# Held loads of v, other engines for copies and adds, and other places for the steps of the front in a fused attention and feed-forward kernel

## The chip, the cores and the metric

The kernel runs on one core of a Trainium2 chip. The metric is the time of one execution in microseconds (us) of device time. Below, TensorE is also called PE (PEld is its weight load), VectorE DVE, ScalarE ACT, GpSimd POOL and SyncE SP, as in the profile.

## What is computed

q, k and v have the shape (8 batches, 8 heads, 576 positions, 64), in float32. Each head has a local attention (a position sees those less than 4 away) and a coarse one (q, k and v averaged over groups of 4 positions, full attention over the 144 groups, the result repeated 4 times). Their sum is the input of a two-layer network with an ELU:

```python
q_d = q.reshape(B, H, Sd, 4, D).mean(axis=3)              # k_d, v_d alike
out_up = np.repeat(sm_attn(q_d, k_d, v_d), 4, axis=2)     # coarse part
scores = np.where(np.abs(pos[:, None] - pos[None, :]) < 4, scale * q @ k.T, -1e9)
out_local = softmax(scores) @ v                           # local part
x = (out_up + out_local).transpose(0, 2, 1, 3).reshape(4608, 512)
h = x @ w_in                                              # 512 -> 2048
out = np.where(h > 0, h, np.exp(np.minimum(h, 0)) - 1) @ w_out   # 2048 -> 512
```

## The kernel before, in words

The attention works on pairs of heads (four pairs, j = 0 to 3, in each batch b), the network on blocks of 512 rows of x (t = 0 to 8). All is issued in one program whose order is written out by hand: `at(time, function, ...)` files a step under a planned time, and at the end (L935) the steps are issued in the order of these times. The times are places in an order, not clock times; each engine then works through its own queue in that order and waits where an input is not there. A move in the tables F, PLAN, MM1 and MM2 therefore moves every instruction of a step in the queues of all engines at once.

The front (tables F and FK, L842 and L843) is batch 0 up to the first matmuls of the network. Its steps are, by the letter of the table:

- T, `first_transposes`: PE transposes q and k of a pair and makes their sums over 4; ACT or DVE copies the four results (qt, kt, qd, kd) out of PSUM. S and Z, `first_scores`: the scores of the first and the second half of the positions, and the exponentials on ACT (0.89 us each).
- V, `first_v`: sums of v over 4 (vs) and their copy (vd). D: denominators and their reciprocals on DVE. P, `first_spread`: the reciprocals spread over the partitions (rb) and copied (rcb).
- O and N: the outputs (lg), scaled on DVE (ln, L568); then the coarse part is added to the local one (L574, on DVE or POOL by a list), which fills x transposed (xt).
- H, `ahead`: the first matmuls of the network (hp, L619). lv, lw, cv: loads of v of batch 0 and 1 and the casts of v (POOL, L242). rp: loads of q and k of batch 1 that cast on the way (POOL's queue, L166). wi: the loads of w_in (POOL's queue, L137). lists `load_wo`: those of w_out (L141).

FK holds numbers of filler matmuls and transposes on zeros (`keep`, L679 and L682), which are issued ahead of a step on PE. Three PSUM tiles (`two`) are passed round between scores, spread reciprocals and outputs, two after `close_front`, so one of these steps waits until the tile of an earlier one has been read.

Then the network runs beside the attention of later batches. mm1 of block 0 is done in 16 parts; each ends in an exponential on ACT (e, L644) and two instructions on DVE (L645 and L646, gt). mm2 (op, L660) needs gt and w_out: the first four groups of four matmuls need the four quarters of w_out in turn. Loads of q, k and v from HBM go through SP's queue, and those with a cast through POOL's. Some loads are held: a memset of one element of the target (L176, L217) makes the load wait until DVE has come to it.

Of the kernel before, what the change touches and what calls it, by code (L numbers as in the profile page):

```python
# [69 lines left out]
def kernel(  # L70
# [9 lines left out]
    nc = tc.nc  # L80
# [131 lines left out]
    def load_v(b, j):  # L212
# [3 lines left out]
        if b == 1:  # L216
            nc.vector.memset(t[0:1, 1, 0:1], 0.0)  # L217
# [346 lines left out]
    def normalise_half(js, g, lg):  # L564
# [7 lines left out]
        for t, a, b_, to in parts:  # L572
            eng = nc.vector if t == 0 and [1, 1, 1, 0, 0, 0, 0, 1][2 * g + js[0] // 2] else nc.gpsimd
# [6 lines left out]
    def normalise(b, j, lg):  # L580
# [14 lines left out]
        while t0 < S * (b + 1):  # L595
# [7 lines left out]
            eng = nc.vector if (b, t) == (1, 1) and [1, 1, 1, 0, 0, 0, 0, 1][4 + j] else nc.gpsimd  # L603
# [80 lines left out]
    def first():  # L684
# [3 lines left out]
        keep(t, 13)  # L688
# [76 lines left out]
    def first_transposes(j, fill):  # L765
        transposes(0, j, fill)
        s, copy = st[(0, j)], dve if [0, 1, 1, 0][j] else act
# [24 lines left out]
    def first_spread(i, n):  # L792
        js, g = halves(i)
        rb = two("rb")
        keep(rb, n)
        spread_half(js, g, rb)
        w = HB + SH
        (dve if [0, 0, 0, 1][i] else act)(
            out=RB[0][:, js[0] : js[1] + 1, w * g : w * g + w], in_=g2(rb[:], 0, w)
        )  # L800

    def first_v(j):
        v_first(0, j, dve if [0, 0, 0, 0][j] else act)
# [38 lines left out]
    F = dict(T=[-41.13, -39.95, -36.66, -32.16], S=[-39.2, -35.63, -33.39, -30.84], Z=[-32.52, -32.14, -32.14, -28.4], V=[-33.32, -30.92, -30.71, -27.94], P=[-29.75, -28.02, -20.88, -18.53], O=[-30, -26.95, -20.73, -13.92], N=[-28.12, -24.72, -19.09, -13.8], H=[-24.18, -20.45, -18.09, -17.91], lv=[-52.45, -36.44, -34.49, -32.17], cv=[-36.2, -33.27, -32.43, -29.76], lw=[-30, -29.11, -20.29, -11.97], rp=[-28.54, -23.88, -22.41, -14.05], D=[-32.62, -29.37, -29.34, -24.56], wi=[-33.19, -32.56, -30.01, -29.05], cf=[-29.29], k=[-41.47, -35.38, -33.37, -28.21])  # L842
    FK = dict(Tq=[1, 0, 0, 0], Tk=[0, 0, 2, 0], S=[1, 0, 2, 1], Z=[1, 0, 2, 0], P=[0, 1, 0, 0], O=[1, 4, 0, 2], D=[0, 0, 0, 0])  # L843
# [29 lines left out]
    MM1 = [[-14.19, 1.09, 0.706], [19.14, 0.992], [35.73, 1.018], [51.52, 1.02]]  # L873
    MM2 = [[14.98, 0.794], [34.5, 1.095], [51.68, 1.02]]
# [13 lines left out]
    def load(n):  # L888
# [5 lines left out]
        1: dict(tr=[-12.21, -5.594, -1.76, -1.482], sc=[-7.07, 0.103, 0.888, 2.276], cast=[-23.96, -13.31, -12.32, 1.701], dn=[16.38], vs=[15.62], sp=[18.61, 18.14, 18.46, 18.98], out=[18.98, 18.52, 18.54, 18.99], so=[10.57], si=[10.03]),  # L894
# [72 lines left out]
```

## Time and profile before

| | us |
|---|---|
| median of 3 runs | 357.72 (356.89 to 359.48) |
| the profiled execution's own time | 356.68 |
| its span, first to last instruction | 354.8 |
| PE busy | 338.6 (95%) |
| DVE busy | 247.1 (70%) |
| ACT busy | 200.0 (56%) |
| POOL busy | 167.6 (47%) |

The profile is one execution. 1.88 us of its time lie outside the span. Times in it are counted from the start of the span. A queue named PEq, SPq and so on is the sequencer of the engine, which waits and issues DMAs. The chain of work is followed back from the last instruction to what released each; "issue" in it is time in which the engine waited for nothing that the profile shows.

### The profile page before, as it was taken

To read this page: it belongs to the slowest core of one execution; us is meant where nothing else is said; L and a number is where in the kernel's file an instruction comes from. 1 tells how busy PE (TensorE), PEld (TensorE's weight loads), DVE (VectorE), ACT (ScalarE), POOL (GpSimd) and SP (SyncE) were. 2 spreads that over 40 slices of the span, in tenths; PEclk is the share of its full clock that TensorE was granted. 3 is DMA by queue.
4 is the path that set the end of the run, shared out by engine and by line. 5 is a ranking of instruction groups with operands and counts; after the bars stand their busy time and mean duration, and the time that the engine had idled before them with its cause. 6 is when DMAs were issued, how large, how long until landed. Compare 5 with 4: busy or idle time off the path is not lost.

```text
span 354.8 us, 8863 instructions
## 1 busy us (share of the span) xinstructions
PE 338.6 (95%) x3520; PEld 191.6 (54%) x3520; DVE 247.1 (70%) x452; ACT 200.0 (56%) x368; POOL 167.6 (47%) x305
## 2 busy tenths in 40 slices
PE   8887998899979999999999999999999999999996
PEld 4665886555555555555555555555555544444443
DVE  2316998676898868887997799879766855555510
ACT  3572798457775754677476736773664444444421
POOL 4534658596877744954595459846200500000000
PEclk9998999999999999999999999999999999999999
DMA  8999999999794958686968698461004010010012
GB/s 180 179 191 200 189 201 217 226 216 229 170 203 92 228 147 164 144 219 152 188 166 217 151 179 202 110 142 35 31 32 117 32 59 30 31 59 30 31 59 89
DMA packets 100322, 49.12 MB, mean 138 GB/s; under 512 B 81770, under 2 KB 95290, under 8 KB 100282
## 3 DMA queue, kind: packets, MB, share of 16 engines
q1 hardware_dynamic: 94442, 42.20, 53.1%
q0 software_dynamic: 5600, 6.26, 10.6%
q8 instruction: 27, 0.44, 0.6%
q10 hardware_dynamic: 240, 0.11, 0.2%
q14 instruction: 13, 0.11, 0.1%
HBM read 42.24 MB, written 9.62 MB: 146 GB/s over the span
## 4 chain that ended last, share of the span: by engine, by line
PE 88%; DVE 5%; ACT 4%; issue 2%; DVEq 0%; ACTq 0%
PE op L660 35%; PE hp L640 31%; PE sc L382 3%; PE lg L531 2%; PE hp L619 2%; PE sc L679 2%; PE tqk L268 2%; ACT pex L402 1%; PE sc L392 1%; PE vs L338 1%; DVE ln L584 1%; DVE gt L646 1%; PE lg L539 1%; PE den L437 1%; ACT e L644 1%
## 5 line engine op out<-in xcount | busy, mean ns | idle before, releaser
L660 PE MATMUL op<-WO,gt 128*128 128x512 f16 (+2 forms) x592 | 145.3, 374 | 0.0
L644 ACT ACTIVATE e<-hp 128x512 f16<-128x512 f32 x144 | 86.3, 602 | 91.8 <-PE hp L640 78.2
L640 PE MATMUL hp<-xt,WI 128*128 128x512 f16 x512 | 132.0, 380 | 0.7 <-DVE xt L604 0.6
L646 DVE SCALAR_TENSOR_TENSOR gt<-hp,e 128x512 f16<-128x512 f32 x144 | 99.6, 692 | 6.4
L660 PEld LDWEIGHTS <-gt 128*128 128x128 f16 x592 | 55.2, 98 | 61.6 <-issue 0.9
L645 DVE TENSOR_SCALAR e<-e 128x512 f16<-128x512 f16 x144 | 60.1, 417 | 40.2 <-ACT e L644 39.5
L640 PEld LDWEIGHTS <-WI 128*128 128x128 f16 x512 | 55.0, 114 | 48.2
L604 POOL TENSOR_TENSOR xt<-ln 128x128 f16<-128x128 f16 (+10 forms) x62 | 37.4, 632 | 48.7 <-DVE ln L591 41.1
L402 ACT ACTIVATE pex<-sc 112x576 f16<-112x576 f32 x112 | 50.0, 528 | 10.6 <-PE sc L392 10.5
L329 POOL TENSOR_TENSOR t<-qt 128x288 f32<-128x288 f16 x27 | 18.2, 672 | 39.4 <-ACT qt L298 39.4
L422 DVE TENSOR_TENSOR pex<-pex,MASK 112x1152 f16<-112x1152 f16 x28 | 23.8, 851 | 15.5 <-ACT pex L402 15.3
L242 POOL CAST v<-v 112x768 f16<-112x768 f32 x32 | 27.0, 844 | 12.2 <-DMA v<-in_v_dram 12.2
L666 ACT COPY os<-op 128x512 f32<-128x512 f32 (+2 forms) x37 | 21.4, 578 | 18.3 <-PE op L660 18.1
L323 DVE TENSOR_REDUCE kd<-kt 128x144 f16<-128x576 f16 x28 | 20.8, 744 | 1.1 <-ACT kt L305 1.1
L298 ACT COPY qt<-tqk 128x576 f16<-128x576 f16 x28 | 18.0, 644 | 5.9 <-PE tqk L268 5.1
L205 POOL CAST k<-k 96x768 f16<-96x768 f32 x24 | 20.4, 848 | 0.1
L205 POOL CAST q<-q 96x768 f16<-96x768 f32 x24 | 19.7, 821 | 0.2 <-issue 0.2
L382 PEld LDWEIGHTS <-kt 64*112 64x112 f16 x336 | 11.3, 127 | 12.4 <-issue 11.6
L619 PE MATMUL hp<-xt,WI 128*128 128x256 f16 x128 | 17.0, 283 | 0.5 <-DVE v L217 0.4
L382 PE MATMUL sc<-qt,kt 64*112 64x96 f16 x336 | 14.7, 217 | 1.5 <-ACT pex L402 1.3
L331 POOL TENSOR_TENSOR qd<-t 128x144 f16<-128x144 f32 x27 | 14.0, 519 | 2.1
L591 DVE TENSOR_TENSOR ln<-lg,rcb 128x576 f16<-128x576 f32 x20 | 15.0, 748 | 0.0
(111 smaller groups left out, 291.5 us busy)
## 6 DMA issues: line engine op xcount, KB each, us to landing
v<-in_v_dram SPq DMA_DIRECT2D x30, 336.0 KB, 6.0
out_dram<-os SPq DMA_DIRECT2D x35, 256.0 KB, 2.1
q<-in_q_dram SPq DMA_DIRECT2D x25, 288.0 KB, 3.5
k<-in_k_dram SPq DMA_DIRECT2D x25, 288.0 KB, 4.3
rcb<-rd SPq DMA_DIRECT2D x10, 360.0 KB, 5.2
WI<-in_moe_w_in_dram POOLq DMA_DIRECT2D x4, 512.0 KB, 9.6
WO<-in_moe_w_out_dram POOLq DMA_DIRECT2D x4, 512.0 KB, 7.8
q<-in_q_dram POOLq DMA_DIRECT2D x7, 144.0 KB, 7.1
```

The costliest lines, as they stand in the source:

```text
L205: nc.gpsimd.tensor_copy(out=x[:], in_=src)
L242: nc.gpsimd.tensor_copy(out=v16[:], in_=v32[:].rearrange("p (e c) d -> p c e d", e=2))
L382: nc.tensor.matmul(sc[e][0:KW, a : a + QB], s["kt"][r, KO - PAD + QB * c :][:, 0:KW], s["qt"][c][r], start=True, stop=True,)
L402: nc.scalar.activation(out=s["p"][0:rows, e, :, a : a + n], in_=g2(sc[0:rows], a, n), func=AF.Exp, scale=SCALE / 16 if b and a == HB else ...
L422: nc.vector.tensor_tensor(out=to, in0=to, in1=mk2, op=AB.mult)
L604: eng.tensor_tensor(out=xt(t)[:, j, t0 - TBLK * t : t1 - TBLK * t], in0=ln[:, la : la + z - a], in1=_rep4(ln[:, ga : ga + (z - a) // 4]), ...
L619: nc.tensor.matmul(FS[i][:, 256 * f : 256 * f + 256], w_in(dc, 2 * n + f), xts[0][:, dc, 256 * h : 256 * h + 256], start=(f == dc == 0), s ...
L640: nc.tensor.matmul(hp, w_in(dc, fc), xts[t][:, dc, :], start=(dc == 0), stop=(dc == DMC - 1),)
L644: nc.scalar.activation(out=e, in_=hp, func=AF.Exp)
L645: nc.vector.tensor_scalar(out=e, in0=e, scalar1=1.0, scalar2=-1.0, op0=AB.min, op1=AB.add)
L646: nc.vector.scalar_tensor_tensor(out=to, in0=hp, scalar=0.0, op0=AB.max, in1=e, op1=AB.add)
L660: nc.tensor.matmul(op_[:, a:z], gts[t][:, fc, 128 * tt : 128 * tt + 128], WO[:, fc, a:z], start=(fc == 0), stop=(fc == FCN - 1),)
```

## The change

- v of batch 0 is now also loaded behind memsets on DVE (L216): its four loads leave SP's queue only when DVE has passed its casts of k of pair 0 and the mask; the fourth memset stands on a buffer that v of pair 0 must have left.
- The adds for the first two outputs (N of index 0 and 1) go from DVE to POOL. The copies of kt, qd and kd of pairs 1 and 2 go from DVE to ACT, those of vd of pairs 0, 1 and 3 from ACT to DVE, and the last copy of rcb of batch 0 from DVE to ACT.
- The steps of the front, of batch 1 and some of batches 2 and 3 get other places, and the fillers other numbers: 15 in place of 13 at the start, 20 transposes in place of 4 ahead of the first transposes, 4 ahead of k's.

In the order that results, PE's queue has T of pairs 0 and 1 first, then S of pair 0, T of pair 2, Z 0, S 1, V 0, Z 1, T 3, S 2, Z 2, D 0, V 1, S 3, O 0, P 0, D 1, Z 3, D 2, V 2, P 1, V 3, D 3, O 1, P 2, O 2, two of H, P 3, two of H, O 3, and then batch 1. POOL's queue has the third and the fourth quarter of w_out later: the fourth stands behind the casts of q, k and v of the first pair of batch 2.

```diff
--- before.py
+++ after.py
@@ -213,7 +213,7 @@
 
         t = V00 if (b, j) == (0, 0) else sb.tile([KW, 2 * NB, D], FP32, tag="v32", bufs=3, name="v32")
         a = v[b, 2 * j]
-        if b == 1:
+        if b < 2:
             nc.vector.memset(t[0:1, 1, 0:1], 0.0)
 
         def part(p0, p1, i0, i1):
@@ -570,7 +570,7 @@
         )
         parts = ((0, 0, HB, 0),) if g == 0 else ((0, 0, TBLK - HB, HB), (1, TBLK - HB, HB, 0))
         for t, a, b_, to in parts:
-            eng = nc.vector if t == 0 and [1, 1, 1, 0, 0, 0, 0, 1][2 * g + js[0] // 2] else nc.gpsimd
+            eng = nc.vector if t == 0 and [0, 0, 1, 0, 0, 0, 0, 1][2 * g + js[0] // 2] else nc.gpsimd
             eng.tensor_tensor(
                 out=xt(t)[:, js[0] : z, to : to + b_ - a].rearrange("p j (u f) -> p j u f", f=4),
                 in0=ln[:, :, a:b_].rearrange("p j (u f) -> p j u f", f=4),
@@ -600,7 +600,7 @@
                 z, t1 = HB, S * b + HB
             h = a // HB if by_pe(b) else 0
             la, ga = (a + SH * h, HB + HB * h + a // 4) if by_pe(b) else (a, S + a // 4)
-            eng = nc.vector if (b, t) == (1, 1) and [1, 1, 1, 0, 0, 0, 0, 1][4 + j] else nc.gpsimd
+            eng = nc.vector if (b, t) == (1, 1) and [0, 0, 1, 0, 0, 0, 0, 1][4 + j] else nc.gpsimd
             eng.tensor_tensor(
                 out=xt(t)[:, j, t0 - TBLK * t : t1 - TBLK * t], in0=ln[:, la : la + z - a],
                 in1=_rep4(ln[:, ga : ga + (z - a) // 4]), op=AB.add,
@@ -685,7 +685,7 @@
         nc.vector.memset(Z[:], 0.0)
         nc.vector.memset(V00[0:PAD, 0, :], 0.0)
         t = two("sc")
-        keep(t, 13)
+        keep(t, 15)
         const(id_np, "ID", nc.scalar)
         load_qk(0, 0)
         for j in range(1, NPAIR):
@@ -764,7 +764,7 @@
 
     def first_transposes(j, fill):
         transposes(0, j, fill)
-        s, copy = st[(0, j)], dve if [0, 1, 1, 0][j] else act
+        s, copy = st[(0, j)], dve if [0, 0, 0, 0][j] else act
         evict_q(0, j, act)
         evict_k(0, j, copy)
         s["qd"] = sb.tile([128, SD], FP16, tag="qd", bufs=4, name="qd")[:]
@@ -795,12 +795,12 @@
         keep(rb, n)
         spread_half(js, g, rb)
         w = HB + SH
-        (dve if [0, 0, 0, 1][i] else act)(
+        (dve if [0, 0, 0, 0][i] else act)(
             out=RB[0][:, js[0] : js[1] + 1, w * g : w * g + w], in_=g2(rb[:], 0, w)
         )
 
     def first_v(j):
-        v_first(0, j, dve if [0, 0, 0, 0][j] else act)
+        v_first(0, j, dve if [1, 1, 0, 1][j] else act)
 
     def first_outputs(i, n):
         lg = FS[(i, 2)] = two("lg")
@@ -839,8 +839,8 @@
 
     at(-100, first)
     at(-65, second)
-    F = dict(T=[-41.13, -39.95, -36.66, -32.16], S=[-39.2, -35.63, -33.39, -30.84], Z=[-32.52, -32.14, -32.14, -28.4], V=[-33.32, -30.92, -30.71, -27.94], P=[-29.75, -28.02, -20.88, -18.53], O=[-30, -26.95, -20.73, -13.92], N=[-28.12, -24.72, -19.09, -13.8], H=[-24.18, -20.45, -18.09, -17.91], lv=[-52.45, -36.44, -34.49, -32.17], cv=[-36.2, -33.27, -32.43, -29.76], lw=[-30, -29.11, -20.29, -11.97], rp=[-28.54, -23.88, -22.41, -14.05], D=[-32.62, -29.37, -29.34, -24.56], wi=[-33.19, -32.56, -30.01, -29.05], cf=[-29.29], k=[-41.47, -35.38, -33.37, -28.21])
-    FK = dict(Tq=[1, 0, 0, 0], Tk=[0, 0, 2, 0], S=[1, 0, 2, 1], Z=[1, 0, 2, 0], P=[0, 1, 0, 0], O=[1, 4, 0, 2], D=[0, 0, 0, 0])
+    F = dict(T=[-42.49, -42.47, -35.86, -31.66], S=[-41.99, -33.35, -31.65, -30.2], Z=[-34.01, -31.74, -30.64, -29.78], V=[-32.96, -30.27, -28.27, -26.71], P=[-29.9, -27.49, -24.5, -19.21], O=[-30, -25.39, -21.5, -14.09], N=[-25.79, -25.13, -21.08, -12.85], H=[-20.09, -19.4, -18.22, -15.07], lv=[-42.59, -39.08, -35.29, -34.59], cv=[-34.12, -33.55, -31.67, -28.48], lw=[-28.68, -26.51, -25.4, -16.37], rp=[-29.81, -21.73, -12.53, -21.96], D=[-30.45, -29.83, -28.52, -25.4], wi=[-32.37, -30.46, -30.45, -30.37], cf=[-29.99], k=[-42.52, -36.01, -30.4, -25.26])
+    FK = dict(Tq=[5, 0, 0, 1], Tk=[1, 0, 0, 0], S=[2, 0, 0, 3], Z=[0, 0, 0, 1], P=[0, 0, 0, 0], O=[0, 2, 0, 1], D=[0, 0, 1, 1])
     for j in range(NPAIR):
         at(F["T"][j], first_transposes, j, (FK["Tq"][j], FK["Tk"][j]))
         at(F["S"][j], first_scores, j, 0, FK["S"][j])
@@ -870,8 +870,8 @@
         spread_four(b, j, rb)
         spread_copy(b, j, rb, copy)
 
-    MM1 = [[-14.19, 1.09, 0.706], [19.14, 0.992], [35.73, 1.018], [51.52, 1.02]]
-    MM2 = [[14.98, 0.794], [34.5, 1.095], [51.68, 1.02]]
+    MM1 = [[-14.06, 1.102, 0.369], [19.14, 0.992], [35.73, 1.018], [51.52, 1.02]]
+    MM2 = [[14.98, 0.794], [34.5, 1.091], [51.68, 1.02]]
 
     def mm1_at(t, i):
         if t == 0:
@@ -891,9 +891,9 @@
             load_v(*pairs[n])
 
     PLAN = {
-        1: dict(tr=[-12.21, -5.594, -1.76, -1.482], sc=[-7.07, 0.103, 0.888, 2.276], cast=[-23.96, -13.31, -12.32, 1.701], dn=[16.38], vs=[15.62], sp=[18.61, 18.14, 18.46, 18.98], out=[18.98, 18.52, 18.54, 18.99], so=[10.57], si=[10.03]),
-        2: dict(tr=[8.521, 19.14, 20.81, 24.84], sc=[16.66, 21.68, 23.15, 26.21], cast=[6.002, 15.82, 19.12, 20.36], dn=[28.71], vs=[29.1], sp=[30.02, 30.15, 29.43, 32.38], out=[30.72, 32.86, 33, 33.03], so=[17.79], si=[28.4]),
-        3: dict(tr=[25.32, 29.24, 30.74, 34.58], sc=[28.69, 32, 36.48, 37.89], cast=[21.15, 25.5, 25.89, 28.85], dn=[40.9], vs=[40.84], so=[41.77], si=[43.95], out=[46.72, 47.24, 48.76, 48.78]),
+        1: dict(tr=[-12.7, -5.731, -3.985, -3.589], sc=[-10.19, -1.15, 1.043, 6.962], cast=[-23.82, -20.64, -11.25, 0.071], dn=[16], vs=[15.84], sp=[18.59, 18.58, 18.58, 18.98], out=[18.98, 18.64, 18.72, 18.98], so=[18.46], si=[18.89]),
+        2: dict(tr=[8.521, 19.14, 20.81, 24.93], sc=[16.66, 21.68, 23.3, 26.36], cast=[6.002, 15.72, 19.12, 20.36], dn=[28.71], vs=[29.1], sp=[30.02, 30.15, 29.43, 32.38], out=[30.72, 32.86, 32.86, 33.03], so=[18.95], si=[33.02]),
+        3: dict(tr=[25.32, 29.24, 30.74, 34.58], sc=[28.69, 32, 36.48, 37.89], cast=[21.15, 25.5, 25.89, 28.85], dn=[40.9], vs=[40.84], so=[41.03], si=[43.42], out=[46.54, 47.06, 48.57, 48.6]),
     }
...
...
@@ -923,9 +923,9 @@
             at(p["si"][0], spread_in, b)
             for js in ((0, 1), (2, 3)) if 2 < b < B - 1 else ((0,), (1,), (2,), (3,)):
                 at(p["out"][js[0]], pair_outputs, b, js)
-    for n, x in enumerate([-8.454, -6.202, 3.581]):
+    for n, x in enumerate([-8.454, -1.338, 4.429]):
         at(x, load, n)
-    for n, x in enumerate([-21.48, -3.996, 1.576, 2.844]):
+    for n, x in enumerate([-23.77, -3.548, -2.09, 7.265]):
         at(x, load_wo, n)
     for t in range(NT):
         for i in range(16):
```

## The prediction

> **What bounds the kernel now.** First the page (busy shares, slices, granted clock):
>
> ```profile
> PE 338.6 (95%) x3520; PEld 191.6 (54%) x3520; DVE 247.1 (70%) x452; ACT 200.0 (56%) x368; POOL 167.6 (47%) x305
> ...
> PE   8887998899979999999999999999999999999996
> ...
> PEclk9998999999999999999999999999999999999999
> ```
>
> PE is the bound, and its work is fixed but for fillers. What can be won or lost lies where its row is under 9: the first third. The windows split this:
>
> ```profile
> 36.38:60.10 23.72, 21.70 (x334) 18.26 (x335) 21.98 (x49) 20.72 (x42) 15.69 (x28) 1.00 1.06 205
> 60.10:73.50 13.40, 11.44 (x203) 7.14 (x201) 8.69 (x15) 5.75 (x10) 8.71 (x19) 1.00 1.13 219
> 73.50:112.00 38.50, 35.23 (x413) 20.48 (x413) 31.90 (x50) 26.34 (x50) 30.20 (x58) 1.00 0.94 193
> 112.00:355.00 243.00, 239.51 (x2034) 124.78 (x2032) 172.02 (x305) 129.71 (x239) 95.42 (x174) 1.00 0.46 111
> ```
>
> The columns are the stretch, then busy time (and instructions) of PE, PEld, DVE, ACT, POOL, granted clock, DMA share, GB/s. From 36.38, where DVE takes up the first ELU (L645), to 60.10, where block 0 is done, DVE is busy 21.98 of 23.72 us: DVE sets the pace, and its idle 1.74 us is all that a better order could win. From 112 on PE hardly waits. So the time moves with the start of that DVE stretch, and with waits of PE up to 73.5. What sets the start is in the chain of waits:
>
> ```profile
> 23.48 1.14 issue
> ...
> 29.13 1.96 issue
> 31.09 0.30 PE den L485 x6
> 31.39 0.97 PE hp L619 x4
> ...
> 41.58 1.03 PE hp L619 x8
> ```
>
> PE stands 1.14 and 1.96 us in the middle of equal matmuls, waiting for no engine. Then four matmuls at L619 take 0.97 us where eight take 1.03 later: the clock was halved (granted 0.83 in 30 to 40 us, so 3.4 us at half). The windows that end inside these two gaps tell what they are:
>
> ```profile
> 17.46:24.00 6.54, 6.01 (x127) 4.24 (x128) 0.00 (x0) 5.48 (x10) 3.75 (x6) 1.00 1.15 184
> 24.00:31.00 7.00, 4.40 (x128) 2.94 (x128) 4.45 (x8) 2.56 (x4) 0.72 (x1) 1.00 1.22 196
> ```
>
> Between the gaps lie 128 matmuls and 128 weight loads, 256 instructions, and as many from 17.46, where PE also stops for 0.03 us. The page's DMA part has 27 packets of kind "instruction", 0.44 MB, so 16 KB each; windows of the DMA view find one at 22.1 to 23.1, just ahead of the first gap's end. I read the gaps as PE waiting for its next 256 instructions, asked for at the last crossing: 7.15 us passed from crossing to crossing the first time (17.46 to 24.61), 6.48 the second (to 31.09).
>
> **The change, part by part.** All against the profiled execution: 356.68 us, of which 354.8 is span; it lies 1.04 under the median of the runs.
>
> *Start.* Before, 13 fillers end at 6.93 and the transposes of pair 0 start at 7.30. Two more fillers cost 0.27 each (two took 0.54 at 15.05) to 0.44 (5.71 / 13); 20 more transposes on zeros (16 ahead of q, 4 ahead of k) 0.069 each (eight took 0.55 at 12.62), 1.4. T 0 ends 1.9 to 2.3 us later; I take 1.9, 10.5 for 8.6. ACT starts on it at 10.1 (before 8.25).
>
> *Copies.* kt, qd and kd of pairs 1 and 2 take ACT about 1.0 us each time (8.88 to 9.9 for pair 0), DVE took 1.19. ACT gains 2.0 us, and 0.76 for rcb, and loses three vd of 0.36: +1.7 on an engine that then works nearly without pause from 10.1. DVE is idle here. Worked through queue by queue with these rows (T 1.4, S or Z 0.62 and an exponential of 0.89 on ACT, V 0.22, D 0.35, P 0.45, O 0.59, four copies 1.4): T 1 at 11.5, T 2 at 14.2, V 0 at 17.0, T 3 at 17.9, S 3 until 22.9, then O 0.
>
> *The held loads.* v of pair 0 leaves SP at 7.5 (mask done at 7.46) for 2.18. Loads of v landed after 5.9 to 14.8 us. At 5.9 it is there at 13.4, cast at 14.25, 2.7 us ahead of V 0. At 9.0, as that load itself took, cast at 17.3: 0.3 us late. I take 0. The two constants behind it on SP, which V 0 and D 0 need, landed at 11.71 and 14.94; moved by the same 5.3 us they come at 17.0 and 20.2, wanted at 17.0 and 20.9: just in time. The copies of k and q landed at 9.1 (pair 1), 11.3 and 13.5, and PE took them at 9.66 after ACT, 12.18 after DVE, and 17.74: none was waited for, so their earlier landing is worth 0 here. v of pair 3 goes out after POOL's cast of pair 0 (14.3; DVE waits for it too, with nothing due behind until V 0), lands near 20.3 by 5.99, and is wanted near 28. Behind it on SP, v of batch 1, pair 0 waits for a memset that now stands behind DVE's second reciprocal: near 26.9, not 17.37. At 8.55 us (the load issued at 26.55) it lands at 35.4; POOL casts it (0.83), and DVE's memset for pair 3, which waits for that cast, stands ahead of the first ELU: DVE can't start before 36.3, against 36.38. At 5.9 us this floor is at 33.6.
>
> *Gaps.* With 28 instructions more, PE crosses in T 3 (near 18.1), in O 0 (23.2) and at the fillers ahead of O 1 (28.8 to 29.4). From the first crossing 6.48 to 7.15 us: the second is open at 24.6 to 25.2, a gap of 1.4 to 2.0; the third at 31.1 to 31.7, a gap near 2.3. Before: 24.61 and 31.09. With shorter reloads they could vanish (bound 0). I take the middle, third at 31.4, +0.3. After it come O 1 with fillers 1.1, P 2 0.45, a wait of 0.45 for the scaled O 1, O 2 0.6, eight of H 1.0, P 3 0.45, eight of H 1.0: first ELU at 36.4 on ACT (35.75 before). **+0.6**. The half clock is taken as before.
>
> *Adds.* DVE took 0.76 us each; POOL took about 0.90 for 128x448 (1.32 for that and a small one), so 1.1 for 576. The first is hidden, H follows 4 us later; the second ends about when P 3 does: 0 to +0.3, taken 0. If the third quarter of w_in weren't there (landings to 31.58, H starts near 34.4), it would cost; it is.
>
> *POOL's queue.* q and k of batch 1, pair 2 are issued at the end of POOL's row of loads and adds, near 43.4 where the last pair went at 37.55. At 4.0 to 7.2 us they land at 47.4 to 50.6; PE wants them near 47.6, and DVE has some 1.5 us in hand. 0 to +1.5; **+0.2**, since the low rows are those not behind a load of w_out. The last quarter of w_out left at 53.50 and landed 8.5 us later, 1.1 ahead of its op at 63.14. Now it stands behind the three casts and marks that followed it (54.02 to 58.40, less its own 0.53): issued near 57.8, at 5.5 (first load of w_in) to 8.5 it lands at 63.3 to 66.3, wanted near 64.4. 0 to +1.9; **+0.5**.
>
> *Outputs of batch 1.* Three P stand together, then two O. rb to the next block's hp took 9.3 us with two groups of op inside (64.24 to 73.5); two copies of 0.91 next to each other and one group of op between: I count 7.9, with one group more ahead. **-0.4** (0 to -1).
>
> Sum +0.6 +0.2 +0.5 -0.4 = +0.9: 357.6 for an execution like the profiled one, 358.6 as a median.
>
> A rule of the Trainium skill speaks against one step. The row: after a gap of 1.96 us, and 1.14 before it, the clock was halved for 3.4 us. "TensorE: Matmul & The Clock Gate", Part 1, has the clock halve only after about 3.4 us idle. By the rule no gap of mine could halve it, and 1.6 us would come back: 357.0. The trace disagrees, so I keep the row.
>
> **Rivals.**
>
> 1. *Reloads come sooner* (faster). v of batch 1 no longer loads from 17 to 27 beside w_in, and later reloads came within 2 to 3 us of the crossing. For it: the gaps are pure waiting, and their 3.1 us and up to 1.7 us of half clock are at stake. Against: w_in lands at 31.6 all the same, and DVE's floor. The start is worth -2.5, and DVE's 1.74 us of slack up to 1 more: 358.6 - 0.6 - 2.5 = 355.5, at the far end 354.
>
> "Runtime: NRT & Kernel Launch", Instruction fetch mechanics, in the Trainium skill calls the cost of a 16 KiB crossing mostly hidden. By that the gaps would not return: 358.6 - 3.1 = 355.5, the same as this rival. The two rows 256 instructions apart speak against it here.
>
> 2. *The half clock twice* (slower). Gaps of 1.7 and 2.3 us lie close; before, 1.14 passed unpunished and 1.96 did not. If the first reaches about 2, another 3.4 us run at half, up to 1.7 us: 360.3, and with w_out late by its bound 361.7.
>
> 3. *Nothing is seen.* DVE's floor holds the start at 36.3, w_out lands in time, the outputs give nothing: 357.7.
>
> **How the numbers follow.** The forecast, a front of little loss and small waits for POOL's loads, 0.40; rival 1 0.18; rival 2 0.22; rival 3 0.20. Time 358.6. The range reaches from rival 1 (355.3) to rival 2 with part of its bound (361.8). About 1%, 3.6 us, is what a measurement can tell: faster than 354.1 is the end of rival 1, 0.08; slower than 361.3 the upper third of rival 2 and the sum of the forecast's upper bounds (0.3 + 1.5 + 1.9), 0.17; within 1% 0.75.
>
> **What would show it.** Right: T 0 ends near 10.5; gaps marked issue in O 0 and ahead of O 1, of 1.4 to 2.3 us; granted clock under 1 about 31; first ELU on DVE 0.3 to 1.2 after 36.4; PE waiting for w_out at its fourth op; POOL's cast of v of batch 1 near 36. Wrong: no gap over 0.5 us before 35; DVE's stretch before 35.5 or after 38.5; a wait of T 2 or V 0 for a DMA; DVE's stretch much shorter or longer than 23.7 us.

## The result, and the profile after

The changed kernel takes 363.9 us (median of 20 executions, 359.4 to 366.3) against 358.4 of the kernel before (20 executions, 355.6 to 362.6): ratio 1.0139, with a 95% interval of 1.0114 to 1.0165. It is slower by more than the 1% that the prediction took for what a measurement can tell, and 2.1 us above the end of the predicted range.

The profiled execution took 365.95 us, span 364.2. It is one of the long ones that the comparison leaves out, so each wait read from it below is also looked for in the profiles of the experiments.

The page of the changed kernel: busy time, PE's slices, granted clock.

```profile
PE 344.0 (94%) x3534; PEld 194.1 (53%) x3534; DVE 245.0 (67%) x450; ACT 201.8 (55%) x372; POOL 168.8 (46%) x307
...
PE   8988798689988999999999999999999999999995
...
PEclk9996999589987999999999999999999999999999
```

PE is busy for 5.4 us longer with only 14 more instructions. The last row shows much of why: the clock was lowered in three places (slices 4, 8 to 9 and 12 to 13, each 9.1 us), before in one. To see what each place cost, both spans are cut at the same five events: first ELU on DVE, first matmul of op, first matmul of block 1's hp (L640), the 64th of these, the end of the last matmul. First the kernel before, then the changed one; the columns are as in the prediction.

```profile
36.38:58.24 21.86, 19.84 (x304) 17.30 (x305) 20.27 (x44) 18.86 (x38) 15.05 (x27) 1.00 1.05 203
58.24:72.09 13.85, 12.49 (x233) 7.76 (x231) 9.02 (x14) 6.43 (x12) 8.15 (x18) 1.00 1.10 220
72.09:110.28 38.19, 34.32 (x404) 19.86 (x403) 31.59 (x50) 26.41 (x50) 29.68 (x57) 1.00 0.99 202
110.28:351.51 241.23, 241.23 (x2046) 125.73 (x2044) 173.70 (x308) 130.55 (x239) 97.14 (x177) 1.00 0.46 111
```

```profile
35.22:58.71 23.49, 19.44 (x305) 17.08 (x302) 21.50 (x44) 19.17 (x39) 17.93 (x32) 1.00 0.93 175
58.71:78.71 20.00, 15.61 (x233) 9.22 (x231) 9.58 (x15) 6.33 (x11) 8.39 (x17) 0.74 1.09 219
78.71:119.11 40.40, 37.13 (x404) 20.82 (x403) 31.60 (x50) 26.42 (x50) 29.20 (x57) 0.92 0.91 175
119.11:360.37 241.26, 241.26 (x2046) 125.86 (x2044) 173.57 (x308) 130.60 (x239) 96.50 (x177) 1.00 0.47 111
```

The instructions are the same (x233, x404, x2046), so the lengths compare directly. The front ends 1.16 us earlier than before. Then 1.63 us are lost in DVE's stretch, 6.15 between the first op and block 1, 2.21 in block 1, nothing after that. The large loss has its cause in the chain of waits of that stretch:

```profile
55.92 0.77 POOL v L242
...
56.98 9.44 DMA WO<-in_moe_w_out_dram
66.42 0.04 issue
66.46 3.57 PE op L660 x8
...
70.77 0.77 ACT rcb L516
71.54 0.04 issue
71.58 0.77 PE rb L508 x6
```

The last quarter of w_out leaves POOL at 56.98, behind the casts of batch 2, pair 0, and takes 9.44 us. PE waits for it for 2.98, and the eight matmuls behind it take 3.57, where eight took 1.89 at full clock. The waits of PE from 36 to 70 us show what else stands there:

```profile
PE op L660 <- DMA WO<-in_moe_w_out_dram: 3.0, 1, 3.0
PE tqk L263 <- DMA q<-in_q_dram: 1.4, 1, 1.4
PE tqk L268 <- ACT pex L402: 1.3, 1, 1.3
PE sc L392 <- DVE kd L323: 0.8, 1, 0.8
PE tqk L263 <- DMA k<-in_k_dram: 0.4, 1, 0.4
```

In the kernel before, the same stretch had two waits of 0.64 (sc, for pex), one of 0.37, and two of 0.3 and less. Last, the front. Timeline lines of PE and DVE (start, length, engine, ..., idle before and its releaser):

```profile
1.19 4.79 PE L679 MATMUL sc<-Z 128*128 128x512 f16 x15 [1.19 <-DVE Z L685]
...
7.96 0.54 PE L279 MATMUL tk<-R,k 96*128 96x144 f16 x6
...
26.94 0.60 PE L679 MATMUL lg<-Z 128*128 128x512 f16 x2 [1.36 <-issue]
...
31.64 0.59 PE L619 MATMUL hp<-xt,WI 128*128 128x256 f16 x2 [0.61 <-issue]
```

```profile
35.22 0.29 DVE L645 TENSOR_SCALAR e<-e 128x512 f16<-128x512 f16 x1 [3.46 <-ACT e L644]
```

Fifteen fillers took less time (4.79) than thirteen had (5.71), which is not a price of the kernel (in the profiles of the experiments thirteen took 4.30 to 5.73, fifteen 4.70 to 5.74). T 0 ended at 8.50, and the two gaps marked "issue" are 1.36 and 0.61 us.

### The profile page after: what moved, and what is told of

The parts are those of the page before. It is cut to its first block, busy times and chain, and to the rows that moved or that the text cites. A ratio compares the mean times of both kernels' runs of the same rounds, so it can differ in the third digit from the quotient of the medians.

```text
span 364.2 us, 8902 instructions
## 1 busy us (share of the span) xinstructions
PE 344.0 (94%) x3534; PEld 194.1 (53%) x3534; DVE 245.0 (67%) x450; ACT 201.8 (55%) x372; POOL 168.8 (46%) x307
## 3 DMA queue, kind: packets, MB, share of 16 engines
q0 software_dynamic: 5600, 6.26, 10.5%
## 4 chain that ended last, share of the span: by engine, by line
PE 81%; DMA 8%; POOL 4%; DVE 3%; ACT 2%; issue 1%; DVEq 0%; POOLq 0%; ACTq 0%
PE op L660 34%; PE hp L640 30%; DMA v<-in_v_dram 3%; PE sc L382 3%; DMA WO<-in_moe_w_out_dram 3%; PE lg L531 3%; DMA k<-in_k_dram 2%; PE tqk L268 2%; PE sc L679 2%; PE lg L539 1%; POOL apart L193 1%; POOL k L205 1%; POOL v L242 1%; PE sc L392 1%; PE vs L338 1%
## 5 line engine op out<-in xcount | busy, mean ns | idle before, releaser
L660 PE MATMUL op<-WO,gt 128*128 128x512 f16 (+2 forms) x592 | 147.4, 378 | 3.0 <-DMA WO<-in_moe_w_out_dram 3.0
L640 PE MATMUL hp<-xt,WI 128*128 128x512 f16 x512 | 133.7, 384 | 0.8 <-DVE xt L604 0.7
L645 DVE TENSOR_SCALAR e<-e 128x512 f16<-128x512 f16 x144 | 61.4, 427 | 45.4 <-ACT e L644 45.1
L640 PEld LDWEIGHTS <-WI 128*128 128x128 f16 x512 | 55.5, 115 | 49.1 <-issue 1.4
L619 PEld LDWEIGHTS <-WI 128*128 128x128 f16 x128 | 13.8, 118 | 2.5 <-issue 1.2
```

The source lines that it names most:

```text
L619: nc.tensor.matmul(FS[i][:, 256 * f : 256 * f + 256], w_in(dc, 2 * n + f), xts[0][:, dc, 256 * h : 256 * h + 256], start=(f == dc == 0), s ...
L640: nc.tensor.matmul(hp, w_in(dc, fc), xts[t][:, dc, :], start=(dc == 0), stop=(dc == DMC - 1),)
L645: nc.vector.tensor_scalar(out=e, in0=e, scalar1=1.0, scalar2=-1.0, op0=AB.min, op1=AB.add)
L660: nc.tensor.matmul(op_[:, a:z], gts[t][:, fc, 128 * tt : 128 * tt + 128], WO[:, fc, a:z], start=(fc == 0), stop=(fc == FCN - 1),)
```

## The experiments

Every kernel was timed in five rounds against the kernel before on the same chip; ratios are to it, with their 95% intervals. Each timed execution also records its mean granted clock, so (1 - clock) x 2 x span is the time it ran at half clock. Over the 122 timed executions of the kernel before that the comparisons use, that was 8.0 us on the mean, and a line through them is 355.3 us + 0.35 us for each us at half clock (5 to 10 us at half: 357.9 on the mean; 10 to 15: 359.4). "Half" below is that mean for a kernel. The changed kernel has 14.4.

### Which half of the change: before_front_of_after and before_rest_of_after

The diff was cut at L860, and each half applied to the kernel before: all of the front (held loads, engines, fillers, F, FK) in one, all behind it (MM1, MM2, PLAN, the loads of batch 2, w_out) in the other.

```diff
-        if b == 1:
+        if b < 2:
...
-        keep(t, 13)
+        keep(t, 15)
```

> The kernel before with the changed front alone (hold, engines, fillers, tables F and FK; the places of batches 1 to 3 and the loads of batch 2 and w_out as before). Theory F: 1.008 or more. Theory Q: 1.005 to 1.010, with PE's wait for q or k of batch 1. Theory W: 0.998 to 1.004, since the network's loads are as before.

Measured 359.0 us, ratio 0.9985 [0.9959, 1.0011], half 8.1.

```diff
...
-    for n, x in enumerate([-8.454, -6.202, 3.581]):
+    for n, x in enumerate([-8.454, -1.338, 4.429]):
...
-    for n, x in enumerate([-21.48, -3.996, 1.576, 2.844]):
+    for n, x in enumerate([-23.77, -3.548, -2.09, 7.265]):
```

> The kernel before with the other half alone (places of batches 1 to 3, loads of batch 2 and w_out, MM1, MM2). Theory W: 1.008 to 1.014, with the wait at the fourth op. Theories Q and F: 0.998 to 1.004.

Measured 362.3, ratio 1.0119 [1.0074, 1.0165], half 13.8. The two longest waits of PE from 40 to 70 us:

```profile
PE tqk L268 <- ACT pex L402: 2.0, 1, 2.0
PE op L660 <- DMA WO<-in_moe_w_out_dram: 1.8, 1, 1.8
```

The front, which the change is named after, costs nothing that can be measured. Theory F falls; the loss is in the other half.

### The last quarter of w_out: after_w_out_early and before_w_out_late

On the changed kernel:

```diff
-    for n, x in enumerate([-23.77, -3.548, -2.09, 7.265]):
+    for n, x in enumerate([-23.77, -3.548, -2.09, 2.844]):
```

> The changed kernel with one number put back: the last quarter of w_out is issued at its place of before (2.844), ahead of the casts of batch 2. Theory W (that load, 2.98 us of waiting at the fourth op and the half clock behind it, up to 1.7 us for each 3.4 us at half, makes most of the loss): ratio to before 1.000 to 1.004, no wait of PE for w_out over 0.3 us, granted clock full from 60 to 80. Theory Q (the casting loads of q and k of batch 1, for which PE waits 1.36 and 0.36 us at 44 to 46, make most of it): still 1.009 or more. Theory F (the front's copies, fillers and reload gaps): still 1.009 or more, with the first ELU of DVE later than before.

Measured 360.1, ratio 1.0044 [1.0010, 1.0077], half 9.9. The window from the first op to block 1, and the group that had waited:

```profile
58.60:72.76 14.16, 11.81 (x232) 7.48 (x230) 9.75 (x15) 6.46 (x12) 8.47 (x17) 1.00 1.18 234
```

```profile
63.30 1.90 PE L660 MATMUL op<-WO,gt 128*128 128x512 f16 x8
```

The quarter was issued at 52.78 and landed at 61.70. The wait is gone, and the window is back from 20.00 to 14.16 (before 13.85). One number takes back two thirds of the loss (1.39 to 0.44%; the intervals do not meet).

On the kernel before:

```diff
-    for n, x in enumerate([-21.48, -3.996, 1.576, 2.844]):
+    for n, x in enumerate([-21.48, -3.996, 1.576, 7.265]):
```

> The kernel before with that one load moved to 7.265. Theory W: PE waits 2 to 4 us at the fourth op, the clock is halved after it, ratio 1.008 to 1.014. Theories Q and F: under 1.005.

Measured 360.7, ratio 1.0045 [1.0016, 1.0073]. Issued at 59.23, the quarter landed after 5.25 us, and in the profile PE did not wait for it. So the late issue alone is not enough for the wait of 3 us: something makes the transfer long too. Theory W's 1.008 and more did not come, and the 0.45% that did came without a wait for w_out in the profile. Half was 11.9, against 8.6 for the kernel before in the same rounds: at 0.35 us each that is 1.2 of the 1.6 us, a fit and not a proof.

### What makes the transfer long: after_load_early and before_w_out_and_loads_late

The changed kernel also moves the loads of q, k and v of batch 2, pair 1 (issued at 47.3 to 48.4 before, 54.2 to 55.2 after), right ahead of the quarter.

```diff
-    for n, x in enumerate([-8.454, -1.338, 4.429]):
+    for n, x in enumerate([-8.454, -6.202, 4.429]):
```

> The changed kernel with one number put back: the loads of q, k and v of batch 2, pair 1, start at -6.202 again instead of -1.338, so near 47 us instead of 54.2; the last quarter of w_out stays late. Theory W2 (the last quarter is late because it is issued late and because its transfer, 9.4 us, shares the DMA engines with these loads; issued as late in the kernel before, with the loads out of its way, it took 5.3): it lands in 5 to 7 us, by 64.5, the matmul that waited 2.98 us for it waits under 0.5, the clock stays full from 60 to 70 us; about 360.3 us, ratio 1.003 to 1.007. Theory W1 (the late issue alone): lands after 65.5, waits over 1.5 us; ratio 1.010 to 1.016. If the wait goes and the ratio stays above 1.010, the wait was not where the time went.

Measured 361.0, ratio 1.0067 [1.0035, 1.0099], half 11.4. The quarter took 7.02 us (59.26 to 66.28):

```profile
66.32 1.89 PE L660 MATMUL op<-WO,gt 128*128 128x512 f16 x8 [1.41 <-DMA WO<-in_moe_w_out_dram]
```

Half of the wait is gone with the loads out of the way, half stays.

Both moves on the kernel before:

```diff
-    for n, x in enumerate([-8.454, -6.202, 3.581]):
+    for n, x in enumerate([-8.454, -1.338, 3.581]):
-    for n, x in enumerate([-21.48, -3.996, 1.576, 2.844]):
+    for n, x in enumerate([-21.48, -3.996, 1.576, 7.265]):
```

> The kernel before with the last quarter of w_out at 7.265 and the loads of batch 2, pair 1, at -1.338, nothing else. Theory W2 (late only together: alone the quarter took 5.25 us and nobody waited): the quarter takes 8 to 10 us, lands after 65.5, TensorE waits 1 to 3 us for it; about 361 to 362 us, ratio 1.007 to 1.011. Rival W1 (the quarter alone cost 0.45 per cent and the loads add nothing): ratio 1.003 to 1.006, wait under 0.5 us.

Measured 361.0, ratio 1.0030 [0.9996, 1.0064]. The transfer took 6.62 us and the wait was there but smaller:

```profile
64.71 1.02 PE L660 MATMUL op<-WO,gt 128*128 128x512 f16 x4 [1.21 <-DMA WO<-in_moe_w_out_dram]
```

The mechanism shows (5.25 us without the loads beside it, 6.62 with them) but not the whole size: on the kernel before, the two moves together cost 0.3%, not the 0.7 to 1.1% I expected. The ratio is the one of rival W1, the wait is not.

In the changed kernel the quarter took 9.4 us, and 9.3 with the changed plan alone. The DMA view from issue to landing shows what lengthens it, for the changed kernel and then for this one:

```profile
DMA packets 2750, 2.38 MB, mean 252 GB/s; under 512 B 1806, under 2 KB 2563, under 8 KB 2749
q1 hardware_dynamic: 2531, 1.60, 70.5%
q0 software_dynamic: 218, 0.76, 40.6%
...
DMA packets 2270, 1.69 MB, mean 255 GB/s; under 512 B 1661, under 2 KB 2141, under 8 KB 2269
q1 hardware_dynamic: 2125, 1.14, 73.1%
q0 software_dynamic: 144, 0.52, 40.7%
```

The columns of the queue lines are packets, MB and the share of the DMA engines' time. The rate is the same, so the time goes with the bytes. POOL's queue (q0) moved 0.52 MB here, which is the quarter alone. In the changed kernel it moved 0.76: the third quarter, issued at 51.85, landed at 59.10, 2.1 us after the fourth was issued; here it had landed at 57.44, before 58.05. For the changed plan issues the second quarter right before the third (at 51.20, before at 47.38; the third leaves at about its old time, 51.8). In after_load_early the third quarter was on its way for 3.0 us beside the fourth, with 0.67 MB of SP's loads (q1) in place of 1.60. These are single profiles, a longer transfer also meets more loads, and no edit moved the second quarter alone.

### The wait or the clock behind it: after_fill_w_out

On the changed kernel, in mm2:

```diff
+        if (t, i) == (0, 3):
+            keep(bank("hp", "fill"), 12)
```

> The changed kernel with 12 matmuls on zeros put ahead of the fourth group of the second projection of block 0, where TensorE waited 2.98 us for the last quarter of w_out. They take 12 x 0.27 = 3.2 us at full clock and leave about as much wait uncovered as the quarter comes later still. Theory C (the wait itself costs little; what costs is the clock, halved for 10.2 us from 65.5 on, in which eight matmuls took 3.57 instead of 1.89 us): the clock stays full there, so up to 5 us come back and at most 0.5 is added: 359 to 361.5 us, ratio 1.001 to 1.007. Theory D (the 2.98 us of waiting are the loss, the half clock falls on work that VectorE paces anyhow): no gain, ratio 1.012 to 1.018.

Measured 363.6 (six executions), ratio 1.0133 [1.0081, 1.0184], half 12.3. The quarter leaves POOL at 57.71 and lands 9.0 us later:

```profile
57.71 0.53 POOL L141 DMA_DIRECT2D WO<-in_moe_w_out_dram  x1
59.93 0.41 PE L268 MATMUL tqk<-ID,q 96*128 96x96 f16 x6 [2.00 <-ACT pex L402]
...
60.44 3.58 PE L662 MATMUL op<-WO,gt 128*128 128x512 f16 x8
...
66.80 2.76 PE L681 MATMUL fill<-Z 128*128 128x512 f16 x12
69.40 1.89 PE L662 MATMUL op<-WO,gt 128*128 128x512 f16 x8
```

The quarter had landed (66.73) when the fillers began (66.80), and the scores ahead of them ended just then. PE was late already, from a wait of 2.00 for ACT's pex and half the clock behind it (3.58 for eight matmuls of op). So in this execution the fillers covered no wait and only cost their 2.6 us. The ratio lies in theory D's range, but the run does not tell theory C from theory D; whether the wait or the clock is the larger part stays open. The clock was halved at 60.4 and again at 74.1.

### The casting loads of q and k of batch 1: after_both

after_w_out_early, and in F:

```diff
-rp=[-29.81, -21.73, -12.53, -21.96]
+rp=[-28.54, -23.88, -22.41, -14.05]
```

> The changed kernel with the last quarter of w_out at its old place (2.844) and the adds of coarse parts with the casting loads of q and k of batch 1 at their old places. Theory Q (the late loads of q and k of batch 1, for which TensorE waited 1.36 and 0.36 us near 45 us, are what is left of the loss once w_out is early): 358 to 359 us, ratio 0.998 to 1.001. Rival (VectorE paces that stretch and these waits cost nothing; the rest is gaps and clock): as with w_out alone early, 1.003 to 1.007, about 360.2 us.

Measured 361.7, ratio 1.0061 [1.0023, 1.0098], against 1.0044 without the second edit. The waits of 1.4 and 0.4 us for q and k are gone from the profile, and nothing is won: other waits set the end of that stretch. Theory Q falls.

### The rest without w_out: before_rest_w_out_as_before

before_rest_of_after, with the quarters at their old places:

```diff
-    for n, x in enumerate([-23.77, -3.548, -2.09, 7.265]):
+    for n, x in enumerate([-21.48, -3.996, 1.576, 2.844]):
```

> The kernel before with the changed numbers behind the front (order of the second block's projections, plans of batches 1 to 3, loads of batch 2) but the four quarters of w_out at their old places. Theory W (the late quarter, beside the moved loads, is what the second half of the change costs): 358 to 359.5 us, ratio 0.998 to 1.003, no wait over 0.5 us for w_out. Rival P (the plans themselves cost, the quarter only adds to it): 361 us or more, ratio above 1.006.

Measured 360.2, ratio 1.0072 [1.0036, 1.0107], half 12.1. No wait for w_out, and yet 0.7%: there is a second cause in the plan. The old places of the quarters are worth 0.47% here (1.0119 to 1.0072, and the intervals meet), half of what they are worth in the changed kernel. The next runs look for it.

### The scores of batch 1, pair 3: after_scores_early and before_scores_late

On the changed kernel, in PLAN[1]:

```diff
-sc=[-10.19, -1.15, 1.043, 6.962]
+sc=[-10.19, -1.15, 1.043, 2.276]
```

> The changed kernel with one number put back: the scores of batch 1, pair 3, at 2.276 instead of 6.962, so one group of eight matmuls of the first projection earlier. Every profile so far with the changed plan shows TensorE idle for 1.2 to 2.35 us ahead of the transposes of batch 2, pair 0, until ACT's exponentials of these scores free their banks; with the old plan two waits of 0.64 us stood ahead of scores instead. Theory S (this wait, and the half clock that comes behind it in several profiles at 59 to 60 us, is part of the loss): the wait of the transposes falls under 0.3, in its place one of about 0.6 ahead of the scores; about 1 to 2 us back, 361.5 to 363 us, ratio 1.007 to 1.011. Rival (ACT's exponentials set that end, the wait only changes its place): no gain, ratio 1.012 to 1.016.

Measured 363.9, ratio 1.0118 [1.0078, 1.0158], half 18.0. The wait only changed its place (0.64 and 0.23 ahead of scores, none ahead of the transposes), and the wait for w_out was there again:

```profile
PE op L660 <- DMA WO<-in_moe_w_out_dram: 3.0, 1, 3.0
PE sc L382 <- ACT pex L402: 0.9, 2, 0.6
```

On the kernel before:

```diff
-sc=[-7.07, 0.103, 0.888, 2.276]
+sc=[-7.07, 0.103, 0.888, 6.962]
```

> The kernel before with the scores of batch 1, pair 3, at 6.962 instead of 2.276 and nothing else. Theory S: a wait of 1.2 to 2.4 us ahead of the transposes of batch 2, pair 0, in place of one of 0.64 ahead of the scores; +0.6 to +2 us, 359.5 to 361 us, ratio 1.002 to 1.006. Rival (the wait only changes its place): ratio 0.998 to 1.002.

Measured 358.7, ratio 1.0004 [0.9969, 1.0039], half 8.1. Both runs speak against theory S, and neither excludes its smaller sizes (the interval here reaches 1.0039, the one above 1.0078). That ACT's exponentials set that end, whichever instruction of PE stands waiting for them, fits both.

### Three put back: after_three_back

```diff
-sc=[-10.19, -1.15, 1.043, 6.962]
+sc=[-10.19, -1.15, 1.043, 2.276]
...
-    for n, x in enumerate([-8.454, -1.338, 4.429]):
+    for n, x in enumerate([-8.454, -6.202, 4.429]):
...
-    for n, x in enumerate([-23.77, -3.548, -2.09, 7.265]):
+    for n, x in enumerate([-23.77, -3.548, -2.09, 2.844]):
```

> The changed kernel with three numbers put back at once: the last quarter of w_out at 2.844, the loads of batch 2, pair 1, at -6.202, the scores of batch 1, pair 3, at 2.276. If these three are the whole loss (theories W2 and S together), it ends where the front of the change alone ended: 358 to 359.5 us, ratio 0.997 to 1.002, no wait over 0.7 us between 45 and 70 us but for q and k of batch 1. If something else of the plans of batches 1 to 3 costs (rival P), 360 us or more, ratio 1.004 to 1.007, as with w_out or the loads put back alone.

Measured 360.4, ratio 1.0049 [1.0013, 1.0085], half 12.1. These three are not the whole loss.

### The outputs of batch 1: before_outputs_moved and after_four_back

On the kernel before, in PLAN[1]:

```diff
-sp=[18.61, 18.14, 18.46, 18.98], out=[18.98, 18.52, 18.54, 18.99]
+sp=[18.59, 18.58, 18.58, 18.98], out=[18.98, 18.64, 18.72, 18.98]
```

> The kernel before with the spreads and outputs of batch 1 as in the changed kernel (three spreads behind each other, then outputs), nothing else. In the profiles with that order TensorE waits 0.70 ahead of the second spread and 0.49 ahead of outputs within one stretch of 3.41 us, which is then busy for 0.65 to 0.70 of the time, and in six of nine of them the clock was halved for 3.4 to 6.8 us from about 70 us on; with the old order the waits lie apart and the shares are 0.74 to 0.83. Theory O (that is the remainder): the order itself gains up to 0.4 us as forecast, the half clock costs 1.4 to 2 in most executions: 359.3 to 360.5 us, ratio 1.003 to 1.007. Rival (as forecast, a gain of 0.4, or nothing): ratio 0.997 to 1.001.

Measured 360.1, ratio 1.0039 [1.0006, 1.0073], half 12.3 against 8.3 for the kernel before in the same rounds. Two stretches of 3.41 us, the second with half the clock:

```profile
66.70:70.11 3.41, 2.22 (x46) 1.52 (x46) 2.72 (x4) 1.80 (x4) 0.00 (x0) 1.00 1.17 230
70.11:73.53 3.42, 3.42 (x45) 1.88 (x44) 1.58 (x2) 0.00 (x0) 2.67 (x6) 0.50 1.23 215
```

The third spread waits 0.70 us for ACT's copy of the first, the second output 0.49 for DVE's copy. Both fall into one stretch in which PE is busy for 2.22 of 3.41 us, and the next one runs at half clock. The extra 4.0 us at half clock times 0.35 are 1.4 us, all of the 0.39%. That is a fit over executions, not an edit that removes the half clock.

after_three_back, and the same two lists put back:

```diff
-sp=[18.59, 18.58, 18.58, 18.98], out=[18.98, 18.64, 18.72, 18.98]
+sp=[18.61, 18.14, 18.46, 18.98], out=[18.98, 18.52, 18.54, 18.99]
```

> The changed kernel with the last quarter of w_out, the loads of batch 2, pair 1, the scores of batch 1, pair 3, and also the spreads and outputs of batch 1 at their old places. Theory O: no half clock from 68 to 76 us, 358 to 359 us, ratio 0.998 to 1.001. Theory P: as with three put back, ratio 1.003 to 1.007.

Measured 358.7, ratio 1.0013 [0.9979, 1.0048], half 7.6. With four of the changed places back, the loss and the additional half clock are gone. Against three put back (1.0049) the outputs are worth 0.36%, as much as alone, though the two intervals meet. In this profile the last quarter, issued early at 51.81, took 10.83 us and PE waited 0.92 for it: a wait of that size need not show in the time.

### The order in the stretch of block 0: before_batch1_plan

On the kernel before:

```diff
-MM1 = [[-14.19, 1.09, 0.706],
+MM1 = [[-14.06, 1.102, 0.369],
-MM2 = [[14.98, 0.794], [34.5, 1.095],
+MM2 = [[14.98, 0.794], [34.5, 1.091],
...
-tr=[-12.21, -5.594, -1.76, -1.482], sc=[-7.07, 0.103, 0.888, 2.276], cast=[-23.96, -13.31, -12.32, 1.701]
+tr=[-12.7, -5.731, -3.985, -3.589], sc=[-10.19, -1.15, 1.043, 6.962], cast=[-23.82, -20.64, -11.25, 0.071]
```

> The kernel before with the changed places of the first projection, the transposes, scores and casts of batch 1, nothing else. Theory P (the order in the stretch of block 0 is the remainder: from the first ELU to the first matmul of the second projection the profiles took 23.3 to 24.2 us with the changed plan, 21.9 to 22.4 with the old one): that stretch takes 23 us or more; 359.5 to 361 us, ratio 1.003 to 1.008. Rival O: the stretch takes 22 to 22.5, ratio 0.998 to 1.002.

Measured 360.0, ratio 0.9991 [0.9944, 1.0037]. The stretch took 22.20 us (37.40 to 59.60), as rival O says, so this order is not what lengthens it. The time is less clear: by the ratio it lies 0.1% under the kernel before, by the medians 0.4% above it (360.0 and 358.6). In this profile PE also waited 1.35 us for the last quarter, issued at its old place, 12.34 us before it landed.

### Two put back: after_w_out_and_outputs_back

after_w_out_early, and:

```diff
-sp=[18.59, 18.58, 18.58, 18.98], out=[18.98, 18.64, 18.72, 18.98]
+sp=[18.61, 18.14, 18.46, 18.98], out=[18.98, 18.52, 18.54, 18.99]
```

> The changed kernel with two numbers lists put back: the last quarter of w_out at 2.844 and the spreads and outputs of batch 1. If these two are the loss (late quarter 0.95 per cent, outputs 0.36 to 0.39, out of 1.39): 358 to 359.2 us, ratio 0.998 to 1.003. Rival (the loads of batch 2 at their new place or the scores cost on their own): ratio above 1.004.

Measured 360.1, ratio 1.0045 [1.0010, 1.0081], half 10.2. My account said 1.000, so it is not finished: with the loads and the scores still moved, the outputs' old order won nothing over after_w_out_early (1.0044). In its profile a wait of 2.10 us for pex and 3.4 us at half clock behind it stand at 56 to 62 us. The 0.4% that w_out leaves cannot be put down to one place; terms of 0.3% with intervals of 0.35 either way do not add up cleanly.

### Fillers against the half clock: before_fill_rb and before_outputs_moved_filled

On the kernel before, in spread:

```diff
+        if (b, j) == (2, 0):
+            keep(rb, 3)
```

> The kernel before with three matmuls on zeros put ahead of the first spreading matmuls of batch 2, near 98 us, where TensorE is idle for 0.75 us; 3 x 0.27 = 0.81 us. Theory K (the clock is granted in stretches of 3.41 us: a stretch in which TensorE was busy for less than about 0.75 of the time can halve the next; over ten profiles the stretches followed by half a clock had 0.29 to 0.76, and most kernels but this one's profile had 3.4 to 6.8 us of half clock from 102 to 113 us, costing some 2 us): no half clock there, so the time is the same as before or up to 2 us better, 356.5 to 358.8, ratio 0.994 to 1.000. Rival (the fillers only delay the work behind them): +0.1 to +0.8 us, ratio 1.000 to 1.003.

Measured 358.4, ratio 1.0038 [1.0008, 1.0069], half 6.9 (as the kernel before beside it). No half clock near 100 us in its profile, but PE still waited 0.74 there: the fillers need the same PSUM tile as the spread and so stood behind the wait, not in it. They cost, as the rival says.

On before_outputs_moved, in spread:

```diff
+        if (b, j) == (1, 2):
+            keep(bank("hp", "fill"), 2)
```

> The kernel before with the outputs of batch 1 moved as in before_outputs_moved, and two matmuls on zeros ahead of the third spread, where TensorE waited 0.70 us for ACT's copy of the first one. They take 0.54 us inside that wait, so nothing is later. Theory K (most of the loss is the clock, halved behind a stretch that was busy for only 0.65): the stretch is then busy for about 0.8, no half clock from 68 to 76 us, and what is left is the waits: 358.6 to 359.6 us, ratio 1.000 to 1.0025. Rival (the waits are the loss): as without the fillers, 1.003 to 1.006.

Measured 360.4, ratio 1.0052 [1.0018, 1.0086], half 13.9. Here the fillers did take the place of the wait of 0.70, and the stretch went from 2.22 to 2.70 us busy:

```profile
65.98:69.40 3.42, 2.70 (x42) 1.74 (x41) 2.38 (x3) 1.60 (x4) 0.85 (x2) 1.00 1.24 190
69.40:72.81 3.41, 3.26 (x40) 1.79 (x41) 1.87 (x3) 0.00 (x0) 2.37 (x5) 0.50 1.25 196
```

The clock was halved all the same. So theory K's cure fails, and its threshold of about 0.75 is too low or not the right measure.

No kernel here beats both: the best, before_front_of_after, cannot be told from the kernel before.

## Why the prediction was wrong

The predicted time was 358.6; measured were 363.9. Of the 1.39% in the changed kernel, 0.95 hang on the last quarter of w_out, and 0.44 stay when it is early.

- **The step that failed: "the last quarter of w_out", +0.5 (0 to +1.9).** Putting it back wins 0.95%, some 3.4 us. Its issue was forecast well (57.8; measured 56.98). Its need came at 63.5 instead of 64.4, and it landed at 66.42, just past the late end of 63.3 to 66.3. So the wait was 2.98, outside the bounds. I had taken the middle of 5.5 to 8.5 us for the transfer. The same change moves the loads of batch 2, pair 1, by 7 us to just ahead of it, and I did not look at what these loads would meet; of a moved load I counted the time of issue and not whom it competes with. With them the transfer took 9.4 us, with them back at their place 7.0. Nor did I see that the third quarter, which I had as moved later too, would still be on its way for 2.1 us in the same queue. The price does not carry over to other surroundings: the late place alone costs 0.45% on the kernel before, and putting all four quarters back wins 0.47% in the second half of the change alone.
- **"The half clock is taken as before"** failed too. It went from 8.0 us on the mean to 14.4; at 0.35 us each that is 2.2 of the 5.0 us. My base was low as well: the profile of the kernel before shows 3.4 us at half clock (granted 0.995), where its executions have 8.0 on the mean.
- **The outputs of batch 1, -0.4**, had the wrong sign. I counted the copies and the op groups and not that the third spread needs the PSUM tile of the first: the window from the first op to block 1 took 14.16 us (after_w_out_early) against 13.85 at full clock, so +0.3, and up to 1.5 with the clock halved (15.34, before_outputs_moved). Alone it cost 0.39%.
- **The start, +1.9 for T 0**, did not come: T 0 ended at 8.50, not 10.5. I had left the thirteen old fillers at the 0.44 us each of one profile; the fifteen took 0.32. In the traces fillers follow each other 0.43 us apart at first and 0.22 apart later, and the moment of the change differs between profiles. On the mean of ten profiles with each front T 0 ended at 7.94 (old) and 8.85 (new), so 0.9 of the 1.9 us is there. **The first ELU**, forecast 0.3 to 1.2 after 36.4, came at 35.22, ahead of the 35.5 that I had called a sign of being wrong. On the mean of the same profiles it came at 37.4 (old) and 35.8 (new). The held v of batch 1 left at 23.16 and landed at 34.30 (26.9 and 35.4 forecast). Alone, the front's forecast of +0.6 us stands against -0.5 (ratio 0.9985, interval -1.5 to +0.4).
- **No copy of k or q was waited for, and the held loads came in time for V 0**: right. v of pair 0 landed at 13.00 (forecast 13.4), and the earlier landing of k and q bought nothing.
- **Gaps**: two, of 1.36 and 0.61, for the forecast "1.4 to 2.0" and "near 2.3". Their size is not fixed by the program: with the same front, other profiles have 1.20 and 3.12 (after_load_early), or one of 4.32 (after_scores_early). On the mean of the ten profiles with each front the gaps together were 3.9 us (old) and 2.3 (new).
- **q and k of batch 1, +0.2**: PE did wait, 1.36 and 0.36 us, and putting the loads back won nothing. The price came out right by luck: other waits set that end, which I had not said.
- **Of the rivals, 2 ("the half clock twice", 361.7 with w_out late by its bound)** came nearest, in sign and in both its ingredients. The front of this profile did have 6.8 us at half clock (27.9 to 34.7) in place of 3.4, as it says; but the front alone has no more half clock than the kernel before (8.1 against 8.6 in the same rounds), and most of the half clock came in the middle and late, behind waits that the second half of the change made. Rival 1 (355.5) was right that the gaps would shrink and the start come earlier (on the mean of the profiles), and wrong that this would show in the time: alone, the front won 0.5 us at best guess and nothing for certain. Rival 3 (357.7) did not happen.

What stays open: how much of the 0.95% is the wait for the quarter and how much the clock behind it, why the same late place costs half as much elsewhere, and which places hold the last 0.4%.

## What to carry to other kernels

When a load is moved, list every other transfer that will be in flight with it at its new place, and take the landing time from rows in which such company was present, not from the middle of all rows. A wait that the schedule creates for a tile or a load can cost twice, once for itself and once for the clock that may be halved behind it; the two were not told apart here. Where the executions of one kernel spread by 2%, read how much of the profiled one ran at half clock before taking it as the base, and do not trust terms of 0.3% to add.

## What the hardware showed that I had not expected

The clock comes in stretches of 3.41 us that do not begin with the program, and the share of a stretch in which PE was busy goes with the grant of the next. Counted over the first 36 such stretches of the 20 profiles here, those at full clock only, shares rounded to hundredths:

| PE's busy share of the stretch | stretches | next at half clock |
|---|---|---|
| under 0.5 | 17 | 17 |
| 0.5 to 0.6 | 11 | 5 |
| 0.6 to 0.7 | 45 | 9 |
| 0.7 to 0.8 | 96 | 14 |
| 0.8 to 0.9 | 65 | 1 |
| 0.9 and more | 367 | 0 |

Two stretches of the changed kernel and the one behind each:

```profile
62.06:65.47 3.41, 1.42 (x20) 0.78 (x19) 1.41 (x2) 1.93 (x5) 2.11 (x5) 1.00 1.04 253
65.47:68.88 3.41, 2.42 (x6) 0.84 (x6) 0.32 (x1) 0.52 (x1) 0.00 (x0) 0.50 1.23 222
...
103.01:106.43 3.42, 2.61 (x47) 1.75 (x46) 3.35 (x5) 2.11 (x3) 3.23 (x8) 1.00 1.22 217
106.43:109.84 3.41, 3.41 (x33) 1.90 (x33) 2.90 (x5) 1.36 (x2) 1.98 (x4) 0.50 1.20 264
```

Neither has an idle time of 3.4 us: the first has 1.99 us idle in all, the second 0.81 spread over several waits. The same work in the kernel before, cut at its own stretches, was busy for 2.56 of 3.42, and the next stretch had the full clock:

```profile
95.96:99.38 3.42, 2.56 (x43) 1.67 (x44) 3.35 (x5) 2.19 (x4) 3.23 (x7) 1.00 1.24 180
99.38:102.79 3.41, 2.84 (x44) 2.02 (x43) 3.38 (x7) 1.39 (x3) 2.29 (x6) 1.00 1.14 262
```

So between 0.5 and 0.8 the busy share does not decide. Part of the spread between executions may be where these stretches happen to fall; that was not tested. The Trainium skill, "TensorE: Matmul & The Clock Gate", Part 1, also has a free-running window of about 3.4 us, which agrees with these stretches; that it takes an idle window, or an idle gap longer than that, does not.

The gaps marked "issue" in the front were also larger than in the profile of before: up to 5.12 us in the middle of the first hp of before_outputs_moved, behind the same front that had 1.96.

```profile
34.60 1.02 PE L619 MATMUL hp<-xt,WI 128*128 128x256 f16 x4 [5.12 <-issue]
```
